# Loading q and k in blocks, placing masks by transfers and spreading softmax sums through memory, in a routed-attention kernel

## The chip, the cores and the metric

The kernel runs on one core of a Trainium2 chip. A core has a matrix engine (TensorE, in the profile PE, with its weight loads as PEld), a vector engine (VectorE, DVE), a scalar engine (ScalarE, ACT), a general engine (GpSimd, POOL) and a queue engine (SyncE, SP) that here issues nearly all transfers between device memory and on-chip memory. Each engine works through its own instructions in order and waits on semaphores for the others. The metric is the device time of one execution in microseconds (us).

## The reference

An attention block is followed by a feed-forward block. Attention has batch 4, 8 heads, sequence 768, head dimension 64. Every query and every key is assigned to the nearest of 16 centroids by cosine similarity, and a query sees only keys of its own cluster:

```python
q_assign = np.argmax(np.einsum('bhsd,hcd->bhsc', q_n, c_n), axis=-1)
k_assign = np.argmax(np.einsum('bhsd,hcd->bhsc', k_n, c_n), axis=-1)
mask = q_assign[:, :, :, None] == k_assign[:, :, None, :]
scores = scale * np.matmul(q, k.transpose(0, 1, 3, 2))
scores = np.where(mask, scores, -1000000000.0)
scores = scores - np.max(scores, axis=-1, keepdims=True)
attn = np.exp(scores)
attn = attn / (np.sum(attn, axis=-1, keepdims=True) + 1e-09)
return np.matmul(attn, v).astype(np.float32)
```

The heads are joined to rows of 512, and the second block computes `x + relu(layernorm(x) * g @ w_ch1) @ w_ch2` with a hidden width of 2048, for 4 x 768 rows.

## The kernel before, in words

The attention stage works on 16 pairs of heads (batch b, pair pr; `pairs`, numbered n). The two heads of a pair lie in the lower and the upper 64 partitions. For each pair there are 12 steps (two halves of 384 queries by six blocks of 128 keys), two steps to a "slot", so six slots (0 to 5) to a pair. In every slot PE computes the scores of two steps (L348: mask products in bf16, then q times k in float32, into `s_ps`), ACT takes the exponential (L341, `e`, five buffers), PE weighs v by the exponentials of two earlier steps (L360, `a_ps`), and DVE adds the exponentials up (`es`, L374 and L377). Scores run one slot ahead: in slot 5 of pair n they already are those of pair n+1, and need its masks.

Around this core the next pair is prepared, slot by slot, in an order written out in the loop (a manual schedule for PE, DVE and ACT; the transfers on SP are placed by the framework's scheduler):

- slot 5 of pair n-2 (for q) and slot 0 of pair n-1 (for k), `prep_transpose`: PE turns six 128 x 128 blocks of the loaded side (L243, `qk_ps`), and ACT copies the two halves out (L249) into `t0` or `t1`. Behind it the next load of that side is issued (L92, `q_sb` and `k_sb`, one buffer each), so that load waits until PE has read the buffer.
- slot 1, `prep_sims`: PE multiplies with the centroids (L260, `sim_ps`); slot 2, `prep_turn` and `prep_route`: PE turns the similarities (L276), DVE finds each token's best centroid (L285) and writes the one-hot rows (L287).
- slot 4, `prep_onehot`: PE turns the one-hot rows (L302, `oh_ps`, 128 partitions in four groups of 32: q and k of both heads), and ACT copies each group to its place in the mask tiles: plain for q (L316), scaled and shifted by a huge number for k (L314).

The pair before is finished alongside, by `finish(n-1, part)`: in slot 1 PE sums `es` over the keys (L397, `den_ps`), ACT copies the result (L405, `dsb`), and four transfers spread one row each over 32 partitions (L407, `rdens`); in slot 3 DVE takes the reciprocal (L409), which is written out as a row (L411, `row`) and read back to all partitions of its head (L419, `rb`); in slot 5 DVE multiplies (L426, `x`), turns 32 x 32 blocks (L433, `y`), and both are written out (L427, L436).

DVE also converts the weights from 64-bit words (`split_weight` and `join_weight`, L209 to L231): two chunks per pair for the first ten pairs, in slots 0 and 3, joined in the slot after, and one per pair from pair 10 on, in slot 0. Statistics of the first batch's rows (L464, L465) run on DVE in pairs 5 to 8, their use (L493, L495) in pairs 10 to 13. The feed-forward stage follows; in it PE runs from end to end.

Of the kernel before, what the change touches and what calls it, by code (L numbers as in the profile page):

```python
# [8 lines left out]
F32 = mybir.dt.float32  # L9
BF16 = mybir.dt.bfloat16  # L10
U32 = mybir.dt.uint32
I32 = mybir.dt.int32
AF = mybir.ActivationFunctionType
# [6 lines left out]
def kernel(  # L20
# [11 lines left out]
    nc = tc.nc  # L32
    B, H, S, D = q.shape
    NCL = centroids.shape[1]
    DM, FF = moe_w_ch1.shape
    P = 128
    NT = S // P
    NHALF = 2
    TH = NT // NHALF
    HC = TH * P  # L40
    Q = 32
# [4 lines left out]
    FAR = 2.0 ** 100  # L46
    WIDE = 1.0e20

    const = ctx.enter_context(tc.tile_pool(name="const", bufs=1))
# [9 lines left out]
    loads = pool("loads", 1)  # L59
    heads = pool("heads", 2)  # L60
    route = pool("route", 1)
    conv = pool("conv", 1)
    attn = pool("attn", 2)
    dram = ctx.enter_context(tc.tile_pool(name="dram", bufs=4, space=bass.MemoryType.DRAM))
# [8 lines left out]
    pairs = [(b, pr) for b in range(B) for pr in range(NPAIR)]  # L73
    loaded = {n: {} for n in range(len(pairs))}

    def load(n, names):
        if n >= len(pairs):
            return
        b, pr = pairs[n]
        for name in names:  # L80

            shape = [P, 2, NT, D] if name == "v" else [P, NT, 2, D]
            t = loads.tile(
                shape, F32, tag=name, name=f"{name}_sb", bufs=2 if name == "v" else 1
            )

            parts = 1 if n or name == "v" else NHALF
            for g in range(parts):
                cs = slice(g * NT // parts, (g + 1) * NT // parts)
                for j in range(2):  # L90
                    queue = nc.scalar if parts > 1 and j else nc.sync
                    queue.dma_start(  # L92
                        out=t[:, j] if name == "v" else t[:, cs, j, :],
                        in_={"q": q, "k": k, "v": v}[name][b, 2 * pr + j].rearrange(
                            "(p c) d -> p c d", p=P
                        )[:, cs, :],
                    )
            loaded[n][name] = t
# [24 lines left out]
    for m in mask[0] + mask[1]:  # L123
        nc.gpsimd.memset(m, 0.0)
    hits = const.tile([P, B * NPAIR], F32, name="hits")
    far = const.tile([P, 1], F32, name="far")
    nc.gpsimd.memset(far, -FAR)

    DE = HC // Q
    rdens = const.tile([P, B * NPAIR, DE], F32, name="rdens")  # L130
# [105 lines left out]
    def prep_transpose(n, side):  # L236
        src = loaded[n]["qk"[side]]
        t_sb = heads.tile([P, S], F32, tag=f"t{side}", name=f"t{side}")
        prepared[n][side] = t_sb
        for g in range(NHALF):  # L240
            t = ps("qk_ps")
            for c in range(TH):
                nc.tensor.transpose(  # L243
                    t[:, c * P : (c + 1) * P],
                    src[:, g * TH + c, :, :].rearrange("p h d -> p (h d)"),
                    ident,
                )
            if g == 0 or n:
                nc.scalar.copy(t_sb[:, g * HC : (g + 1) * HC], t[:, :HC])  # L249
            else:  # L250
                nc.vector.tensor_copy(t_sb[:, g * HC : (g + 1) * HC], t[:, :HC])
# [45 lines left out]
    def prep_onehot(n):  # L297
        t = ps("oh_ps", BF16, 1024)
        for g in range(NHALF):
            for c in range(TH):  # L300
                o = (g * TH + c) * P
                nc.tensor.transpose(  # L302
                    t[:, o : o + P],
                    onehot[:, c, g, :, :, :].rearrange("p s j d -> p (s j d)"),
                    identb,
                )

        for side in range(2):
            m = mask[n % 2][side]
            for j in range(2):  # L310
                src = t[(side * 2 + j) * Q : (side * 2 + j + 1) * Q, :S]
                dst = m[j * D : j * D + Q, :]
                if side:
                    nc.scalar.activation(dst, src, AF.Identity, bias=far[:Q], scale=FAR)  # L314
                else:
                    nc.scalar.copy(dst, src)  # L316
            prepared[n]["m", side] = m

# [69 lines left out]
    def finish(n, part):  # L390
        b, pr = pairs[n]
        if part == 0:
            den = ps("den_ps")
            for j in range(2):
                for g in range(NHALF):
                    r = (j * NHALF + g) * Q
                    nc.tensor.matmul(  # L397
                        den[r : r + Q, :HC], ones, sums[n, g][:, j, :],
                        start=True, stop=True, tile_position=(0, r),
                    )  # L400
            if n + 1 < len(pairs):
                dsb = last.tile([P, HC], F32, tag="dsb", name="dsb", bufs=1)
            else:
                dsb = late["all"][:, 1, :HC]
            nc.scalar.copy(dsb, den[:, :HC])  # L405
            for r in range(0, P, Q):
                nc.sync.dma_start(out=rdens[r : r + Q, n, :], in_=dsb[r : r + 1, :])  # L407
        elif part == 1:
            nc.vector.reciprocal(rdens[:, n, :], rdens[:, n, :])  # L409
            row = dram.tile([2, S], F32, tag="row", name="row")  # L410
            nc.sync.dma_start(  # L411
                out=row.rearrange("j (p e) -> (j p) e", e=DE), in_=rdens[:, n, :]
            )
            if n + 1 < len(pairs):
                rb = last.tile([P, S], F32, tag="rb", name="rb", bufs=1)
            else:
                rb = late["all"][:, 2]
            for j in range(2):
                nc.sync.dma_start(  # L419
                    out=rb[j * D : (j + 1) * D, :],  # L420
                    in_=row[j : j + 1, :].to_broadcast([D, S]),
                )
            late[n] = rb
        else:
            x = xs.pop(n)
            nc.vector.tensor_tensor(x, x, late.pop(n), ALU.mult)  # L426
            nc.sync.dma_start(out=xT_d[b][pr], in_=x)  # L427

            if n + 1 < len(pairs):
                y = last.tile([P, S], F32, tag="y", name="y")  # L430
            else:
                y = late["all"][:, 2]
            nc.vector.transpose(y, x)  # L433
            for i in range(P // Q):
                m = pr * P + i * Q
                nc.sync.dma_start(  # L436
                    out=x_d[b].rearrange("t (a r) m -> r (t a) m", r=Q)[:, :, m : m + Q],
                    in_=y[i * Q : (i + 1) * Q].rearrange("r (g f) -> r g f", f=Q),
                )
# [4 lines left out]
    rows = {}  # L444
# [117 lines left out]
    with tc.manual_schedule(engines=order):  # L562
        prep_transpose(0, 0)
        load(1, "q")
        turn_centroids()
        prep_transpose(0, 1)
        load(1, "k")
        prep_sims(0)
        scores(0, "qk", ("qk",))
        prep_turn(0)  # L570
        scores(1, "qk", ("qk",))
        prep_route(0)
        prep_transpose(1, 0)
        load(2, "q")
        load_weight(0)
        load_weight(1)
        prep_onehot(0)
        scores(0, "qk", ("mask", "exp"))
        scores(1, "qk", ("mask", "exp"))
        for u in range(len(pairs) * slots):  # L580
            n, slot = divmod(u, slots)
            nxt = n + 1 < len(pairs)
            if slot == 1:
                load(n + 1, "v")
            if slot == 0 and nxt:
                prep_transpose(n + 1, 1)
                load(n + 2, "k")
            if slot == 1 and nxt:
                prep_sims(n + 1)
            if slot == 2 and nxt:  # L590
                prep_turn(n + 1)
                prep_route(n + 1)
            if slot == 4 and nxt:
                prep_onehot(n + 1)
            if slot == 5 and n + 2 < len(pairs):
                prep_transpose(n + 2, 0)
                load(n + 3, "q")
            if slot == 1 and n:
                finish(n - 1, 0)
            for i in (2 * u + 2, 2 * u + 3):  # L600
                if i < len(steps):
                    scores(i)
            weigh(2 * u)
            weigh(2 * u + 1)
            if slot == 3 and n:
                finish(n - 1, 1)
            if slot == 5 and n:
                finish(n - 1, 2)
            if (n, slot) in convert:
                split_weight(convert[n, slot])  # L610
            if (n, slot - 1) in convert:
                join_weight(convert[n, slot - 1])
                load_weight(convert[n, slot - 1] + 2)
            for job in extra.pop((n, slot), ()):
                job()
# [446 lines left out]
```

## Time and profile before

| | us |
|---|---|
| median of 3 runs | 979.47 (978.92 to 980.03) |
| the profiled execution | 979.16 |
| its span in the trace | 977.4 |
| PE busy | 954.9 |
| DVE busy | 640.4 |
| ACT busy | 329.7 |

The profiled time is the device's own; the span runs from the first instruction of the trace to the last. The chain of waits is followed back from the last instruction: 90% of it lies on PE. Busy time is the sum over a whole execution, and attention and feed-forward use the engines differently, so the shares are to be read stage by stage. The attention stage ends at about 390 us. Of the weights, transfers and other rows of the page the prediction shows what it uses.

### The profile page before, as it was taken

Reading aid. Unit: us, or ns where it says so; the run is one execution under the profiler, and the core shown is the slowest. Engines: PE = TensorE matmul, PEld = TensorE weight load, DVE = VectorE, ACT = ScalarE, POOL = GpSimd, SP = SyncE. Lnnn points to the kernel's source line nnn. Section 1 sums busy time; section 2 is a strip of 40 time slices with the busy share of each in tenths; the row PEclk is TensorE's granted clock in tenths of the full one; section 3 lists DMA queues with packets and bytes.
Section 4 is the critical chain, followed back from the end, with each engine's and each line's share of the span. In section 5 each row is a group of like instructions: output and inputs, shape, how many; then the busy total and the mean of one; then the engine's idle time right before and its main releaser. Section 6 shows DMA issues by size and latency. Waiting matters only on the chain.

```text
span 977.4 us, 12727 instructions
## 1 busy us (share of the span) xinstructions
PE 954.9 (98%) x4758; PEld 593.5 (61%) x4758; DVE 640.4 (66%) x1206; ACT 329.7 (34%) x525; POOL 4.9 (1%) x31
## 2 busy tenths in 40 slices
PE   5999999999999999999999999999999999999997
PEld 3444444444444443556888556888556888556886
DVE  2788888998877777799874455653455564455431
ACT  4666676677676676222000221000211000221000
POOL 2000000000000000000000000000000000000000
PEclk9999999999999999999999999999999999999999
DMA  6346656665654422432542000212000221000011
GB/s 162 88 126 167 171 156 188 165 170 153 153 141 119 119 73 60 113 98 75 171 119 72 6 0 1 97 60 71 0 1 6 92 69 62 1 1 6 28 39 40
DMA packets 141445, 84.01 MB, mean 86 GB/s; under 512 B 110608, under 2 KB 127040, under 8 KB 141376
## 3 DMA queue, kind: packets, MB, share of 16 engines
q1 hardware_dynamic: 139104, 82.70, 30.5%
q8 instruction: 39, 0.64, 0.3%
q10 hardware_dynamic: 2272, 0.43, 0.2%
q14 instruction: 30, 0.25, 0.1%
HBM read 64.00 MB, written 19.00 MB: 85 GB/s over the span
## 4 chain that ended last, share of the span: by engine, by line
PE 90%; ACT 5%; issue 2%; DVE 1%; DMA 1%; ACTq 0%; SPq 0%; DVEq 0%
PE x_ps L737 17%; PE x_ps L652 17%; PE s_ps L348 14%; PE a_ps L360 12%; PE z_ps L737 8%; PE z_ps L652 8%; PE y_ps L737 4%; PE y_ps L652 4%; ACT mask_0k L314 1%; ACT mask_1k L314 1%; PE qk_ps L243 1%; ACT e L341 1%; PE sim_ps L260 1%; PE den_ps L397 1%; DMA q_sb<-in_q_dram 1%
## 5 line engine op out<-in xcount | busy, mean ns | idle before, releaser
L341 ACT ACTIVATE e<-s_ps 128x768 f32<-128x768 f32 x192 | 151.8, 817 | 55.2 <-PE s_ps L348 51.7
L348 PE MATMUL s_ps<-t,t 64*128 64x384 f32 x768 | 156.9, 487 | 0.0
L377 DVE TENSOR_TENSOR es<-es,e 128x768 f32<-128x768 f32 x128 | 122.3, 955 | 39.0 <-ACT e L341 32.4
L360 PE MATMUL a_ps<-e,v_sb 128*64 128x384 f32 x768 | 144.8, 499 | 0.0
L360 PEld LDWEIGHTS a_ps<-e,v_sb 128*64 128x64 f32 x768 | 46.7, 136 | 86.4 <-issue 86.3
L737 PE MATMUL x_ps<-w2t,h 128*128 128x256 f32 x384 | 84.5, 379 | 0.0
L348 PEld LDWEIGHTS s_ps<-t,t 64*128 64x128 f32 x768 | 69.4, 190 | 19.8 <-issue 19.7
L737 PEld LDWEIGHTS x_ps<-w2t,h 128*128 128x128 f32 x384 | 72.7, 190 | 10.1
L667 ACT COPY u<-x_ps 128x384 f32<-128x384 f32 x64 | 30.7, 479 | 134.2 <-PE x_ps L652 134.2
L667 ACT COPY p<-x_ps 128x384 f32<-128x384 f32 x32 | 15.3, 479 | 139.3 <-PE x_ps L652 139.3
L530 DVE TENSOR_TENSOR ws<-w 128x256 f32<-128x256 f32 x64 | 24.8, 418 | 53.3 <-PE z_ps L652 53.3
L748 DVE TENSOR_TENSOR o_sb<-x_ps,xb 128x256 f32<-128x256 f32 x48 | 20.2, 420 | 54.5 <-PE x_ps L737 54.5
L672 DVE TENSOR_TENSOR h<-z_ps,u 128x384 f32<-128x384 f32 x64 | 35.2, 550 | 22.4 <-ACT u L667 13.8
L652 PE MATMUL x_ps<-xn,w 128*128 128x384 f32 x128 | 46.6, 487 | 0.6 <-ACT late L386 0.6
L652 PE MATMUL z_ps<-xt,ws 128*128 128x384 f32 x128 | 46.6, 487 | 0.0
L652 PE MATMUL x_ps<-xt,w 128*128 128x384 f32 x128 | 46.6, 487 | 0.0
L652 PE MATMUL x_ps<-xt,ws 128*128 128x384 f32 x128 | 46.5, 486 | 0.0
L652 PE MATMUL x_ps<-xn,ws 128*128 128x384 f32 x128 | 46.5, 486 | 0.0
L652 PE MATMUL y_ps<-xn,w 128*128 128x384 f32 x128 | 46.5, 486 | 0.0
L652 PE MATMUL z_ps<-xn,ws 128*128 128x384 f32 x128 | 46.5, 486 | 0.0
L737 PE MATMUL x_ps<-w,h 128*128 128x256 f32 x192 | 42.7, 379 | 0.0
L737 PE MATMUL y_ps<-w,h 128*128 128x256 f32 x192 | 42.1, 379 | 0.0
(130 smaller groups left out, 1309.0 us busy)
## 6 DMA issues: line engine op xcount, KB each, us to landing
raw<-in_moe_w_ch_dram SPq DMA_DIRECT2D x32, 512.0 KB, 3.9
v_sb<-in_v_dram SPq DMA_DIRECT2D x32, 192.0 KB, 3.8
xn<-xT_d SPq DMA_DIRECT2D x16, 384.0 KB, 4.7
xr<-x_d SPq DMA_DIRECT2D x24, 256.0 KB, 3.3
xb<-x_d SPq DMA_DIRECT2D x48, 128.0 KB, 2.2
out_dram<-o_sb SPq DMA_DIRECT2D x48, 128.0 KB, 1.7
q_sb<-in_q_dram SPq DMA_DIRECT2D x30, 192.0 KB, 3.9
k_sb<-in_k_dram SPq DMA_DIRECT2D x30, 192.0 KB, 3.5
```

The source lines that it names most:

```text
L243: nc.tensor.transpose(t[:, c * P : (c + 1) * P], src[:, g * TH + c, :, :].rearrange("p h d -> p (h d)"), ident,)
L314: nc.scalar.activation(dst, src, AF.Identity, bias=far[:Q], scale=FAR)
L341: nc.scalar.activation(e, s[:, :, :HC], AF.Exp, scale=SCALE)
L348: nc.tensor.matmul(s[:, j, :HC], of_keys[rows[j], keys], of_queries[rows[j], cols], start=part == first, stop=part != first, skip_group_ch ...
L360: nc.tensor.matmul(acc[j * D : (j + 1) * D, :HC], loaded[n]["v"][:, j, c, :], e[:, j, :], start=(c == 0), stop=(c == NT - 1),)
L377: nc.vector.tensor_tensor(es, es, soft.pop(i), ALU.add)
L530: nc.vector.tensor_tensor(t[:, i], x, y, op)
L652: nc.tensor.matmul(bank[:, :HC], lhs[:, c, :], rhs[:, c, :], start=first and c == 0, stop=c == NDH - 1, skip_group_check=True,)
L667: nc.scalar.copy(t, bank[:, :HC])
L672: nc.vector.tensor_tensor(h, bank[:, :HC], other, ALU.add)
L737: nc.tensor.matmul(bank[:, :MH], hidden[lhs + (c,)][:, tt * P : (tt + 1) * P], rhs[:, c, :], start=first and c == 0, stop=c == NFH - 1, sk ...
L748: nc.vector.tensor_tensor(o, bank[:, :MH], x, ALU.add)
```

## The change

Three things change, all in the attention stage, and one call moves.

1. `load_blocks`: k of pairs 1 to 15 and q of pairs 10 to 15 (21 sides) are loaded by four transfers, each of 32 partitions by 24 runs of 32 numbers (128 bytes), so that a DVE transpose of 32 x 32 blocks gives the same `t0` or `t1` that PE and ACT gave. Before, a side was loaded by two transfers in runs of 256 bytes. For these sides `prep_transpose` is one DVE instruction.
2. `prep_onehot` copies all 128 partitions out in one ACT instruction, with a bias and a scale that differ by partition (`far` has two columns now), and four transfers put 16 rows each in the mask tiles. It is called in slot 3 instead of slot 4.
3. `finish`, part 0: the four rows are written to device memory by one transfer (`flat`), and read back by a second one to 128 partitions by 12.

```diff
+    blocks = {(n, name) for n in range(1, len(pairs)) for name in ("qk" if n >= 10 else "k")}
+
+    def load_blocks(n, name):
+        b, pr = pairs[n]
+        t = loads.tile([P, S], F32, tag=name, name=f"{name}_sb")
+        for i in range(P // Q):
+            nc.sync.dma_start(
+                out=t[i * Q : (i + 1) * Q].rearrange("f (t a r) -> f t a r", t=NT, r=Q),
+                in_={"q": q, "k": k}[name][b, 2 * pr + i * Q // D].rearrange(
+                    "(a f t) d -> f t a d", f=Q, t=NT
+                )[:, :, :, i * Q % D : i * Q % D + Q],
+            )
+        loaded[n][name] = t
...
+        if (n, "qk"[side]) in blocks:
+            nc.vector.transpose(t_sb, src)
+            return
...
+        m = route.tile([P, S], BF16, tag="m", name="m")
+        nc.scalar.activation(m, t[:, :S], AF.Identity, bias=far[:, 0:1], scale=far[:, 1:2])
         for side in range(2):
-            m = mask[n % 2][side]
             for j in range(2):
-                src = t[(side * 2 + j) * Q : (side * 2 + j + 1) * Q, :S]
-                dst = m[j * D : j * D + Q, :]
-                if side:
-                    nc.scalar.activation(dst, src, AF.Identity, bias=far[:Q], scale=FAR)
-                else:
-                    nc.scalar.copy(dst, src)
-            prepared[n]["m", side] = m
+                o = (side * 2 + j) * Q
+                nc.sync.dma_start(
+                    out=mask[n % 2][side][j * D : j * D + NCL, :], in_=m[o : o + NCL, :]
+                )
+            prepared[n]["m", side] = mask[n % 2][side]
...
-            for r in range(0, P, Q):
-                nc.sync.dma_start(out=rdens[r : r + Q, n, :], in_=dsb[r : r + 1, :])
+            flat = dram.tile([P // Q, HC], F32, tag="flat", name="flat")
+            nc.sync.dma_start(out=flat, in_=dsb[0:P:Q, :])
+            nc.sync.dma_start(
+                out=rdens[:, n, :], in_=flat.rearrange("i (p e) -> (i p) e", e=DE)
+            )
...
-            if slot == 4 and nxt:
+            if slot == 3 and nxt:
                 prep_onehot(n + 1)
```

The framework's scheduler places the transfers on SP. In the built programs the transfers issued while pair 4 runs stand in this order, before and after:

```
before: rdens x4, raw, xn, row, rb x2, raw, q_sb x2, xT_d, x_d x4, k_sb x2, v_sb x2
after:  flat, raw, mask q, rdens, mask q, mask k x2, q_sb, row, q_sb, xn, rb x2, raw,
        v_sb x2, xT_d, x_d x4, k_sb x4
```

More of the change, by code (lines that the diff above doesn't have):

```diff
@@ L80, in load @@
         for name in names:
+            if (n, name) in blocks:
+                load_blocks(n, name)
+                continue
             shape = [P, 2, NT, D] if name == "v" else [P, NT, 2, D]
@@ L125 @@
     hits = const.tile([P, B * NPAIR], F32, name="hits")
-    far = const.tile([P, 1], F32, name="far")
-    nc.gpsimd.memset(far, -FAR)
+    far = const.tile([P, 2], F32, name="far")
+    for rows, bias, scale in ((slice(0, D), 0.0, 1.0), (slice(D, P), -FAR, FAR)):
+        nc.gpsimd.memset(far[rows, 0:1], bias)
+        nc.gpsimd.memset(far[rows, 1:2], scale)
     DE = HC // Q
```

## The prediction

> **What bounds the kernel now.** I read the busy shares first, then the chain that ended last, then one attention pair on the timeline, and last the transfer queue. The whole-kernel shares say that TensorE (PE) is busy 98% of the time. They are an average over two stages, and only the attention stage (to about 390 us) is touched.
>
> ```profile
> PE 954.9 (98%) x4758; PEld 593.5 (61%) x4758; DVE 640.4 (66%) x1206; ACT 329.7 (34%) x525; POOL 4.9 (1%) x31
> DVE  2788888998877777799874455653455564455431
> ```
>
> The reader should see that VectorE (DVE), which gets new work, is 80 to 90% busy in slices 3 to 11, far above its mean of 66%. The chain of waits then shows one "turn" (first mask product of a pair to that of the next):
>
> ```profile
> 112.04 1.79 PE s_ps L348 x12
> 113.83 1.44 PE a_ps L360 x8
> 115.27 0.81 PE qk_ps L243 x6
> ...
> 119.24 0.78 PE sim_ps L260 x8
> 120.02 0.65 PE den_ps L397 x8
> ...
> 123.83 0.48 PE simT_ps L276 x3
> ...
> 135.41 1.79 PE s_ps L348 x12
> ```
>
> A turn is 135.41 - 112.04 = 23.37 us, nearly all PE. On the timeline (starts up to 0.07 earlier) it splits into six score steps of 1.72, six weighings of 1.44, turning k 0.81, similarities and denominators 1.43, their turn back 0.48, one-hot 0.44, turning q 0.88, and a wait of 0.37: sum 23.37. DVE and the queue in that turn:
>
> ```profile
> 114.94 0.98 DVE L433 STREAM_TRANSPOSE y<-x 128x768 f32<-128x768 f32 x1
> 115.84 0.92 DVE L374 TENSOR_TENSOR es<-e 128x768 f32<-128x768 f32 x1
> 121.24 2.79 SPq L407 DMA_DIRECT2D rdens<-dsb  x4
> 124.34 0.56 DVE L285 TENSOR_REDUCE best<-simT_ps 128x24 f32<-128x384 f32 x1 [1.74 <-PE simT_ps L276]
> 128.22 0.22 DVE L409 RECIPROCAL rdens<-rdens 128x12 f32<-128x12 f32 x1
> 128.47 0.33 SPq L411 DMA_DIRECT2D row<-rdens  x1
> 129.93 1.13 SPq L419 DMA_DIRECT2D rb<-row  x2
> 135.07 0.59 SPq L92 DMA_DIRECT2D q_sb<-in_q_dram  x1
> 135.39 0.96 DVE L377 TENSOR_TENSOR es<-es,e 128x768 f32<-128x768 f32 x1 [1.16 <-ACT e L341]
> 135.41 0.34 PE L348 MATMUL s_ps<-mask_1q,mask_1k 64*128 64x384 bf16 x2 [0.37 <-ACT e L341]
> ```
>
> DVE waits only 1.74 + 1.16 = 2.90 us per turn, so it works 20.47. The reciprocal L409 runs four microseconds after its four transfers were issued, without waiting, and row leaves the queue before the next q load.
>
> **The change, part by part.**
>
> *Removed from PE.* Turning k, 0.81 in every turn. For pairs 10 on also turning q, 0.88 (two pairs ahead, so from turn 8 on). The 0.37 wait goes too: the exponential at its end stands behind four mask copies (131.11 to 134.53, 3.4 us of ScalarE), which become one of 0.90 (the 895 ns of a 768-column copy; more partitions, same columns) a slot earlier. PE alone would then need 23.37 - 0.81 - 0.37 = 22.19 us a turn, and 21.31 once q is off it as well.
>
> *Added to DVE.* A turn of one side costs 0.90, the distance from y's start to the next start above. DVE then works 21.37 of 22.19 us: it fits only if it waits less than 0.82 us per turn. So every new wait on DVE counts.
>
> *Block loads.* Each side becomes four issues of 128-byte runs instead of two of 256. The nearest row is x_d<-y, same shape outwards, 0.55 per issue and 2.6 us to landing. Bounds for the load are 2.6 and, doubling today's 3.9, 7.8. Either lies under the turn (over 20 us) between load and use: cost nothing. If that cover were gone, the DVE turn would wait for it.
>
> *Sums by two transfers.* The write to flat follows the copy of den as today and has 5 us of cover. The read rdens<-flat is what matters. In the order in which the changed kernel issues its transfers (a listing of the built program, no times) it stands behind the first mask transfer from pair 2 on, except in pair 5. That transfer waits for the mask copy, which waits for the one-hot product. So L409 waits for a product of slot 3 (of 0 to 5), and behind L409 on DVE stand the conversion of weights, four sums, the x product, y, and now the turn of k, for which PE's similarities wait. That closes a loop, similarities to similarities:
> - PE to the one-hot: 1.43 + 3.16 + 0.48 + 3.16, and 0.55 until ScalarE starts (130.56 to 131.11): 8.78.
> - Mask copy 0.90, queue 0.03, one mask issue 0.59.
> - rdens<-flat to landing: nearest below is row<-rdens (same 128 x 48 bytes, outwards) at 1.4, nearest above rb<-row (a read of rows just written, 32 times the bytes) at 3.3. I take 1.9, nearer to the row of its size.
> - DVE, from starts in the timeline: reciprocal 0.14, split 1.34, two sums 1.93, join 2.52, two sums 1.94, x 0.98, y 0.90, k 1.02: 10.77.
>
> Together 22.97, plus 0.82 for each batch-norm statistic in between (0.68 + 0.17, less overlap), plus 0.90 where q is turned on DVE too.
>
> *The q load moves past row and rb.* In the listing rb<-row stands behind the q load (pairs 2 to 6), in pairs 3 and 4 row itself as well. The q load waits until PE has turned the former q at slot 5. Similarities to there: 1.43 + 3.16 + 0.48 + 3.16 + 0.44 + 3.16 + 3.16 + 0.88 = 15.87. Then a q issue 0.59, row to rb 1.46 (128.47 to 129.93), second rb issue 0.54, landing 3.3, and x, y, k 2.90: 24.7. Bounds: row at 1.4, or 2.5 if its packets queue behind q's as some rdens rows do (1.7 to 3.8 today); I take the idle value. Where row goes first, two q issues stand ahead of rb: 15.9 + 1.2 + 0.54 + 3.3 + 2.90 = 23.85.
>
> *Masks by transfer.* Copy done at 9.7 of that loop's time, five issues of 0.58, landing 2.0 as rdens: ready at about 14.1, needed at 15 or later. Cost nothing, 0.9 of slack where q is on DVE; a landing of 3.8 would add 0.9 per turn there. In the prologue there is no slack: 0.90 + 1.74 + 2.0 against 3.43 is +1.2, less 1.47 of k on PE, plus 0.90 on DVE: +0.6 (from -0.3 to +2).
>
> [...] By stretches (PE and its weight loads, DVE, ACT, POOL busy, then the granted clock):
>
> ```profile
> 15.50:20.70 5.20, 1.86 (x16) 1.23 (x16) 0.00 (x0) 4.11 (x6) 0.00 (x0) 1.00 0.44 99
> 20.70:24.10 3.40, 3.40 (x15) 2.19 (x16) 1.80 (x3) 2.27 (x5) 0.00 (x0) 0.50 0.06 13
> ```
>
> After 5.2 us with 1.86 us of PE work the clock is halved for 3.4 us. [...]
>
> **The sum** (15 turns, number n starts with pair n):
> - turn 0: +0.6
> - turns 1, 2 at 22.19: 2 x -1.18 = -2.4
> - turn 3 at 23.85: +0.5; turns 4, 5 at 24.7: +2.7
> - turns 6, 7 at 24.7 (23.85 plus a statistic; the first loop with two gives 24.6): +2.7; turn 8 at 24.6: +1.2; turn 9 (statistic and q) at 24.7: +1.3; turn 10 at 24.2 (q, small work): +0.8, less 0.1 that before lost here
> - turns 11 to 14: one conversion (3.86) gone from the loop, so PE's 21.31 decides: 4 x -2.06 = -8.2
> - last pair and feed-forward: +0.2; one more transfer, feed-forward work of 20 us over it.
>
> Net -0.7. The profiled execution took 979.16 us (span 977.4, 1.8 around it), 0.3 under the median of 979.47. The forecast is 979.16 - 0.7, or 978.4 us: no change that can be told (0.2%, or 2 us, is about what a measurement of this kernel tells from none).
>
> **Rivals.**
> - *The relief comes through* (PE decides everywhere): turns 1 to 7 at 22.19, 8 to 14 at 21.31: 7 x -1.18 + 7 x -2.06 + 0.7 = -22, 957 us. For it: 2.9 us of DVE waiting today. Against: 0.82 is left, and two new waits stand ahead of k. Partial relief ends at 960 to 970.
> - *The spread read lands late* (slower): rdens<-flat at 3.3 instead of 1.9 lengthens turns 7 to 10 by 1.4 each, and pushes turns 11 to 14 to about 22.3 (+1.0 each): +9.6, 988 us. It decides from about 2.4 (+0.5 in eight turns). For it: it is a read of rows just written, as rb is, in a queue that is busier. Against: 6 KB only.
> - *The k wait hits less often* (same side, small gain): middle turns (4 to 10) at 24.1 instead of 24.6 give 7 x -0.5, or 975.
>
> **How the numbers follow.** Cancelling as summed, 0.53 (own range 972 to 985; 0.20 faster, 0.20 same, 0.13 slower); relief 0.11; k wait rarer 0.07; late read or a tripped clock 0.29, of which 0.02 still same. So faster 0.38, same 0.22, slower 0.40. The range goes to 968 (half of the relief kept) and 991 (late read, with some row queueing).
>
> **What would show it.** Right: similarities (sim_ps) wait 1.5 to 3.4 us for the DVE turn of k in turns 3 to 10 and not in 11 to 14; L409 waits for rdens; turns of 22.2, then 24 to 25, then 21.3. Wrong: no such waits (relief), PE waiting for masks, or a granted clock below 1 in the middle turns.

## The result, and the profile after

The changed kernel takes 1010.69 us (median; 1009.92 to 1012.09) against 979.19 us of the kernel before in the same runs: a ratio of 1.0324, interval 1.0306 to 1.0341. It is 31.5 us slower. The forecast was 978.4 with a range up to 991, so both the time and the range were missed. The profiled execution took 1012.09 us (span 1010.3).

The page of the changed kernel, its busy times, the granted clock by slice, and the shares of the chain:

```profile
PE 961.8 (95%) x4632; PEld 583.1 (58%) x4632; DVE 658.6 (65%) x1227; ACT 277.6 (27%) x435; POOL 5.1 (1%) x34
PEclk9999998999999999999999999999999999999999
PE 77%; DMA 9%; DVE 8%; SPq 2%; ACT 2%; issue 1%; ACTq 0%; DVEq 0%
```

PE had 126 matmuls fewer (4632 against 4758) and was still busy 6.9 us longer: some of them ran at a granted clock of 0.50, and in the turns with a wait the similarities run in two parts, as shown below. Before, 90% of the chain that ended last lay on PE and 1% on transfers; now it is 77% and 9%, with 8% on DVE. The waits of PE and of DVE say where (us in total, times, longest):

```profile
PE sim_ps L283 <- DVE t L261: 30.7, 12, 5.3
PE s_ps L370 <- DMA mask_0k<-m: 4.5, 1, 4.5
...
DVE rdens L434 <- DMA rdens<-flat: 29.4, 11, 4.8
DVE x L451 <- DMA rb<-row: 29.2, 12, 5.6
```

DVE, which waited for no transfer inside a turn before, now stands 58.6 us at two small transfers, the read of the denominators and that of `rb`, and PE stands 30.7 us at the turn of k that is queued behind them. (In the changed kernel L261 is DVE's turn of a side, L283 the similarities, L434 the reciprocal, L451 and L458 x and y, L336 the mask transfers, L429 and L430 the write and the read of the denominators, L436 row, L444 rb, L83 and L110 the loads.)

By turn, in us (forecast: the prediction's; half clock: an estimate, half of PE's busy time in the stretches of granted clock 0.50 behind the wait):

| turn | forecast | measured | wait for the turn of k | lost to half clock |
|---|---|---|---|---|
| 0 | 23.1 | 22.59 | | |
| 1, 2 | 22.19 | 22.13, 22.13 | | |
| 3 | 23.85 | 25.03 | 2.08 | |
| 4, 5 | 24.7 | 30.65, 30.35 | 5.33, 4.68 | 2.5, 2.8 |
| 6, 7 | 24.7 | 27.96, 27.97 | 3.37, 3.58 | 1.7, 1.5 |
| 8, 9 | 24.6, 24.7 | 26.33, 27.83 | 2.58, 3.80 | 1.7, 1.4 |
| 10 | 24.2 | 23.60 | 1.45 | |
| 11 | 21.31 | 26.19 | 2.41 | 1.7 |
| 12, 13, 14 | 21.31 | 22.72, 22.72, 22.45 | 0.57, 0.58, small | |

The turns together took 380.65 us, 31.8 more than the forecast's 348.9. Of these 13.3 are half clock, by that estimate; 18.5 are a turn of k that comes later than forecast. The start was 1.4 us later than before, the rest of the kernel 0.7 longer.

The column of waits counts idle time alone, and a turn with a wait is some 0.8 us longer still. PE runs the similarities of q, has nothing more to do until k is turned, and then runs those of k; before, they ran side by side. So turn 3, at a granted clock of 1.00, has 22.95 us of PE work against 22.13 in turns 1 and 2, and with its wait of 2.08 that makes 25.03. Turns 4 to 7 have 22.85 to 22.89 us of work once the half clock is taken off, which agrees.

Turn 4 shows the loop through rb, on the timeline:

```profile
112.79 0.62 SPq L110 DMA_DIRECT2D q_sb<-in_q_dram  x1
113.46 0.64 SPq L436 DMA_DIRECT2D row<-rdens  x1
114.14 0.59 SPq L110 DMA_DIRECT2D q_sb<-in_q_dram  x1
114.78 0.64 SPq L474 DMA_DIRECT2D xn<-xT_d  x1
116.31 1.12 SPq L444 DMA_DIRECT2D rb<-row  x2
122.30 0.96 DVE L451 TENSOR_TENSOR x<-x,rb 128x768 f32<-128x768 f32 x1 [4.64 <-DMA rb<-row]
123.29 0.98 DVE L458 STREAM_TRANSPOSE y<-x 128x768 f32<-128x768 f32 x1
124.20 0.94 DVE L261 STREAM_TRANSPOSE t<-k_sb 128x768 f32<-128x768 f32 x1
125.19 0.85 PE L283 MATMUL sim_ps<-t,cT 128*32 128x384 f32 x2 [5.33 <-DVE t L261]
```

The q loads and xn stand ahead of rb, as forecast; the two rb reads, issued from 116.31 on, had landed at 122.3, 5.4 us after the second issue, where the kernel before shows 3.3. The stretches in which rb is under way, before, in this turn and in turn 9 (length, busy times, clock, busy share of the transfer engines, GB/s):

```profile
129.90:134.30 4.40, 4.40 (x33) 1.84 (x30) 4.13 (x6) 3.29 (x5) 0.00 (x0) 1.00 0.27 91
```

```profile
116.30:122.30 6.00, 3.56 (x22) 1.08 (x18) 1.25 (x2) 1.77 (x3) 0.00 (x0) 1.00 0.91 272
256.60:260.50 3.90, 3.90 (x28) 1.87 (x26) 3.69 (x7) 2.25 (x4) 0.00 (x0) 1.00 0.31 103
```

The transfer engines were 27% busy under the old rb and 91% under this one. The wait of turn 9, where rb is not behind q, shows the other loop; it starts in turn 8, which ends at 255.96:

```profile
245.61 0.38 SPq L220 DMA_DIRECT2D raw<-in_moe_w_ch_dram  x1
250.75 0.58 SPq L336 DMA_DIRECT2D mask_1q<-m  x1
251.43 0.53 SPq L430 DMA_DIRECT2D rdens<-flat  x1
254.89 0.23 DVE L434 RECIPROCAL rdens<-rdens 128x12 f32<-128x12 f32 x1 [4.80 <-DMA rdens<-flat]
264.41 0.95 DVE L451 TENSOR_TENSOR x<-x,rb 128x768 f32<-128x768 f32 x1
266.30 0.94 DVE L261 STREAM_TRANSPOSE t<-k_sb 128x768 f32<-128x768 f32 x1
267.29 0.85 PE L283 MATMUL sim_ps<-t,cT 128*32 128x384 f32 x2 [3.80 <-DVE t L261]
```

SP stood almost five microseconds (from 245.99 to 250.75) at the mask transfer, which waits for ACT's copy; the read of the denominators was issued behind it, and DVE reached its reciprocal 3.5 us after that issue. Everything behind L434 on DVE moved with it, down to the turn of k.

And the half clock. The trace records a granted clock of 0.50 behind seven of the waits for the turn of k: for 6.83 us from 123.28 and from 154.00 (turns 4 and 5), and for 3.41 us from 184.72, 212.03, 239.34, 266.64 (turns 6 to 9) and 317.84 (turn 11). Stretches of turns 4, 10 and 11 (columns as above, PE busy first, the clock third from the end):

```profile
119.87:123.28 3.41, 0.00 (x0) 0.00 (x0) 0.96 (x1) 0.00 (x0) 0.00 (x0) 1.00 0.79 272
123.28:126.70 3.42, 1.51 (x10) 0.58 (x12) 3.37 (x5) 0.00 (x0) 0.00 (x0) 0.50 0.70 179
126.70:130.10 3.40, 3.40 (x15) 1.42 (x12) 3.26 (x6) 1.33 (x3) 0.00 (x0) 0.50 0.89 138
290.50:293.95 3.45, 2.00 (x18) 0.55 (x16) 3.42 (x5) 0.49 (x2) 0.00 (x0) 1.00 0.98 192
314.43:317.84 3.41, 1.00 (x12) 0.40 (x12) 3.41 (x5) 0.01 (x1) 0.00 (x0) 1.00 0.79 188
317.84:321.25 3.41, 3.41 (x14) 1.45 (x12) 3.27 (x6) 1.55 (x3) 0.00 (x0) 0.50 0.85 136
```

Behind the stretch without PE work (from 119.87) and the one with 1.00 us of it (turn 11) the clock was 0.50; behind the one with 2.00 us (turn 10) it stayed at 1.00. In turn 4, where the wait reaches into the half clock, PE was busy for 1.51 us of its first 3.42 and the clock was 0.50 for another 3.40; in turn 11 PE was busy all through the 3.41 us, and the clock behind them was 1.00.

### The profile page after: what moved, and what is told of

Same layout as the page of the kernel before. It is cut to its first block, busy times and chain, and to the rows that moved or that the text cites. A ratio compares the mean times of both kernels' runs of the same rounds, so it can differ in the third digit from the quotient of the medians.

```text
span 1010.3 us, 12513 instructions
## 1 busy us (share of the span) xinstructions
PE 961.8 (95%) x4632; PEld 583.1 (58%) x4632; DVE 658.6 (65%) x1227; ACT 277.6 (27%) x435; POOL 5.1 (1%) x34
## 4 chain that ended last, share of the span: by engine, by line
PE 77%; DMA 9%; DVE 8%; SPq 2%; ACT 2%; issue 1%; ACTq 0%; DVEq 0%
PE x_ps L762 16%; PE x_ps L677 16%; PE s_ps L370 9%; PE z_ps L762 8%; PE z_ps L677 8%; PE a_ps L382 7%; PE y_ps L762 4%; PE y_ps L677 4%; DVE es L399 2%; DMA q_sb<-in_q_dram 2%; DMA rdens<-flat 2%; DMA raw<-in_moe_w_ch_dram 2%; PE sim_ps L283 2%; PE den_ps L419 1%; DMA rb<-row 1%
## 5 line engine op out<-in xcount | busy, mean ns | idle before, releaser
L370 PE MATMUL s_ps<-t,t 64*128 64x384 f32 x768 | 161.7, 500 | 0.0
L370 PEld LDWEIGHTS s_ps<-t,t 64*128 64x128 f32 x768 | 71.9, 197 | 24.0 <-issue 24.0
L283 PE MATMUL sim_ps<-t,cT 128*32 128x384 f32 x128 | 28.3, 577 | 30.8 <-DVE t L261 30.7
```

The costliest lines, as they stand in the source:

```text
L283: nc.tensor.matmul(sim[r : r + Q, :HC], cT[:, pr, :, :].rearrange("p j c -> p (j c)"), prepared[n][side][:, g * HC : (g + 1) * HC], start= ...
L370: nc.tensor.matmul(s[:, j, :HC], of_keys[rows[j], keys], of_queries[rows[j], cols], start=part == first, stop=part != first, skip_group_ch ...
```

## Experiments

**Theory 1:** the work is cheap enough, but the turn of k stands on DVE behind x and the reciprocal, which now wait for small transfers that stand behind other things on SP's queue; the half clock behind such waits adds to it. **Theory 2:** the work itself is too much: DVE full, loads in small pieces slow, or SP's many issues too long. Each run is compared with the kernel before, measured beside it (979.0 to 979.8 us).

### The parts one by one

`no_blocks` keeps the masks by transfer and the two-transfer sums, and loads and turns all sides as before; `blocks_only` is the reverse (masks, sums and the slot of `prep_onehot` as before).

```diff
-    blocks = {(n, name) for n in range(1, len(pairs)) for name in ("qk" if n >= 10 else "k")}
+    blocks = set()
```

> The changed kernel without its first part: all sides of q and k loaded whole and turned by PE as before; masks by one copy and transfers in slot 3, sums by two transfers. Theory 1, the two other parts do no harm as long as no turn stands on VectorE: the 0.37 us wait of 14 turns goes, the prologue loses 1 to 2: 973 to 978 us. Theory 2, the transfers of masks and sums are what costs: over 985 us.

> The first part of the change alone: 21 sides in blocks and turned on VectorE, masks by four copies in slot 4 and sums by four transfers as before. Theory 1, the turn of k behind x, and x behind rb, is enough for the loss because the scheduler again puts rb behind the loads of q (and from pair 10 on row behind a load of v): waits of sim_ps in most turns, 1000 to 1035 us. Theory 2, the loss needs the read rdens<-flat behind the mask transfers: no waits over 1 us, 958 to 970 us.

Measured: `no_blocks` 974.57 us (ratio 0.995, 0.9934 to 0.9967), in theory 1's range, turns of 22.93; `blocks_only` 1058.21 us (1.0802, 1.0779 to 1.0825). So masks and sums together are a small gain, 0.44 us a turn, and the blocks carry the loss. `blocks_only` was also worse than the whole change, further than I had expected. Its waits:

```profile
DVE x L447 <- DMA rb<-row: 77.1, 11, 9.7
PE sim_ps L281 <- DVE t L259: 58.8, 11, 8.3
```

```profile
SPq L110 <- PE a_ps L381: 74.0, 6, 14.6
```

The last line is SP's: a load of v waits for its buffer, until PE has used the v before, and in turns 9 to 14 of this program the scheduler had put `row` behind that load. The same DVE instruction is late for another reason, also an order on SP's queue.

### The same instructions, transfers in written order

`sp_written` takes nothing away; SP joins the engines whose order is the program's.

```diff
-    order = {mybir.EngineType.PE, mybir.EngineType.DVE, mybir.EngineType.Activation}
+    order = {mybir.EngineType.PE, mybir.EngineType.DVE, mybir.EngineType.Activation, mybir.EngineType.SP}
```

> Same instructions as the changed kernel, but the transfers on SP are issued in the written order of the loop (rdens in slot 1, masks, row and rb in slot 3, the q load in slot 5) instead of the scheduler's. Theory 1, the order of the queue puts rdens, row and rb late, and the turn of k on VectorE stands behind them: the waits of sim_ps for the turn of k (30 us in 13 turns now) all but go, turns of 22.1 and then 21.3 us, full clock after the prologue, 956 to 962 us. Theory 2, VectorE has too little room (21.4 of 22.2 us) and the longer landings alone are enough: waits of over 1 us stay in most turns, over 980 us.

Measured: 982.78 us (1.0029, 1.0014 to 1.0043). 28 of the 31 us go by order alone, which is theory 1's direction; theory 2's number (over 980) held too, because more than 20 us of the expected relief did not come. PE's waits in the attention stage show why:

```profile
PE s_ps L370 <- DMA mask_0k<-m: 10.3, 2, 8.2
PE s_ps L370 <- DMA mask_1k<-m: 5.6, 2, 5.0
PE sim_ps L283 <- DVE t L261: 1.4, 3, 0.6
```

The wait for the turn of k has shrunk from 30.7 to 1.4 us. Now mask transfers are late, behind loads: 8.2 us at the start, 2.1 and 5.0 us at the ends of turns 5 and 10, each with half clock behind it (a mean granted clock of 0.85 in turn 0, 0.93 in turn 6, 0.89 in turn 11).

### Needless work ahead of the similarities

```diff
-                nc.tensor.matmul(
+                for _ in range(9 if 4 <= n <= 12 and side == 0 else 1):
+                    nc.tensor.matmul(
...
```

> The changed kernel, with 3.1 us of needless matrix work (16 repeated products of the q side's similarities, overwritten) ahead of the similarities of k in turns 3 to 11, where PE waits now. Theory 1, the halved clock after those waits costs about 15 us of its own: the halved stretches after the prologue (31 us in seven turns) go, 992 to 999 us, although PE has more to do. Theory 2, the clock does not matter because VectorE's chain sets the pace: 1008 to 1015 us.

Measured: 1051.18 us (1.0732, 1.0714 to 1.075). The run missed its aim. I had sized the filler by the four similarities of a pair (eight records in the profile), which run side by side in 0.67 us. Nine that write the same group of 32 partitions run one after another: turns 3 to 7 were 31.81 us, which is 22.13 + 9.68, or 0.605 for each of the 16 extra ones, and not 3.1 for all (turns 8 to 11, without the turn of q on PE, were 31.0 to 31.3):

```profile
112.00:143.81 31.81, 31.81 (x187) 12.97 (x183) 20.66 (x32) 13.24 (x20) 0.00 (x0) 1.00 0.51 124
```

PE is busy throughout, at a granted clock of 1.00: with that much room no transfer and no DVE instruction made it wait in turns 3 to 11. It doesn't separate the half clock from the waits, as it was meant to. The order on SP differed too (rb ahead of q), so nothing more is drawn from it.

### The turn of k ahead of x

`k_early` moves the turn of k from slot 0 of the pair before to slot 5 of the one before that, beside that of q, ahead of x and y.

```diff
-            if slot == 0 and nxt:
+            if slot == 0 and n == 0:
...
                 prep_transpose(n + 2, 0)
                 load(n + 3, "q")
+                prep_transpose(n + 2, 1)
+                load(n + 3, "k")
```

> The changed kernel with VectorE's turn of k moved from the first step of a pair to the last step of the pair before, ahead of x and y, which wait for rb. Theory 1 (the 31 us are PE waiting for a turn of k that stands behind x's wait for rb): the 30 us of waits ahead of the similarities in turns 3 to 13 go, and with them the stretches at half clock; VectorE's own work of 22 to 24 us sets those turns: 962 to 978. Theory 2 (it is not the place of the turn: the transfers of k and q in pieces land late, or VectorE has too much work): the wait moves to the den products or to the turn itself, 990 or more.

Measured: 991.38 us (1.0127, 1.0109 to 1.0146). The time lies in theory 2's range, at its edge, but the wait is not where theory 2 put it. The similarities wait no more, as theory 1 says, and what is queued next behind x, the one-hot rows, takes their place:

```profile
PE oh_ps L325 <- DVE onehot L310: 19.1, 9, 3.6
```

```profile
DVE rdens L434 <- DMA rdens<-flat: 20.1, 12, 3.2
DVE x L451 <- DMA rb<-row: 18.9, 11, 4.9
```

DVE's standing at the two transfers is the cause, and the turn of k was only the first thing behind it. In turns 12 and 13 this kernel reached 21.32 us.

### Masks off SP's queue

`masks_pool` issues the mask transfers from GpSimd, in the scheduler's order otherwise; `spw_masks_pool` does it with SP in written order.

```diff
-                nc.sync.dma_start(
+                nc.gpsimd.dma_start(
                     out=mask[n % 2][side][j * D : j * D + NCL, :], in_=m[o : o + NCL, :]
                 )
```

> The changed kernel with the four mask transfers of a pair issued by GpSimd instead of SyncE, so that the read of the denominators no longer stands behind a transfer that waits for ScalarE's copy of the masks. Theory 1a (that place in the queue, the loop through masks, denominators, x and the turn of k, makes most of the waits): turns 9 to 14 fall from 145 us together to about 134, and turns 3 to 8 keep some of theirs from rb behind q: 975 to 1000. Theory 1b (the place of rb behind the loads of q, v and xn alone is enough to keep VectorE late): within 8 us of 1010 or above it.

> SyncE's transfers in their written order and the masks from GpSimd: no small transfer stands behind a load, and no mask behind a wait. Theory 1: what the run in written order still lost (mask products waiting 8.2, 2.1 and 5.0 us, with the half clock behind them) goes; turns of 22.2 throughout: 955 to 966. Theory 2 (the parts together give no more than the masks and sums alone, 974.6): 972 or more.

Measured: `masks_pool` 1065.02 us (1.0868, 1.085 to 1.0887), `spw_masks_pool` 977.51 us (0.9974, 0.9958 to 0.9991). The first fell on theory 1b's side, and far beyond: rb stayed behind the loads of q in turns 4 to 8, and in turns 9 to 14, with the masks gone, the scheduler put a v load ahead of row, and SP stood at it:

```profile
SPq L110 <- PE a_ps L382: 74.4, 8, 14.5
```

So a queue's order can't be changed here at one place alone. The second lies in theory 2's range and above theory 1's, but not for theory 2's reason: its turns 10 and 12 to 14 were 21.32 us, PE's floor, but 8.5 us were still waited for masks at the start, and up to 3.3 us for the turn of k, as DVE still stood 7.8 us at rb and 6.7 at the denominators.

### Loads in whole rows

`spw_rows_dve` is `sp_written` with the 21 sides loaded by two transfers in runs of 256 bytes. DVE turns what it finds, so that q and k are out of order, and only the time is of use.

```diff
-            if (n, name) in blocks:
-                load_blocks(n, name)
-                continue
...
-            nc.vector.transpose(t_sb, src)
+            nc.vector.transpose(t_sb, src.rearrange("p a b c -> p (a b c)"))
```

> Written order as before, masks on SyncE, but the 21 sides are loaded in whole rows by two transfers, as the kernel before loads them, and VectorE turns what it finds, so that q and k are not the reference's: the turn costs the same, only the form of the load differs. Theory 1 (the pieces of 128 bytes cost SyncE's time, four issues instead of two, and nothing else): 2 us less on the queue ahead of the masks, whose waits shrink: 970 to 980 against 982.8. Theory 2 (small pieces slow every other transfer): 955 to 966.

Measured: 977.93 us (0.9983, 0.9973 to 0.9992), a step of 0.9983 against 1.0029, or 4.5 us. That lies in theory 1's range. Which part of the 4.5 us is SP's shorter issue and which the transfer engines' was not separated.

### x and y two slots later

`x_late` moves x and y of a pair from slot 5 to slot 1 of the next pair, two slots on (the expectation calls them steps).

```diff
-            if slot == 5 and n:
+            if slot == 1 and n > 1:
+                finish(n - 2, 2)
+            if slot == 5 and n + 1 == len(pairs):
                 finish(n - 1, 2)
```

> The changed kernel with one move: x and y of a pair (VectorE's product with rb and its turn) come two steps later, behind the next turn of k and its similarities, instead of right ahead of it; the transfers stay in the order that the scheduler gives them. Theory 1 (the waits of PE come from the turn of k standing behind x, which waits for rb): the 30 us of waits and the stretches at half clock of the middle turns go, also the loop through masks and denominators, since the masks no longer hang on x: 957 to 972. Theory 2 (SyncE's queue, with its 14 to 18 us of issues in a turn, is late by itself, and something else of it reaches PE): 985 or more, with PE waiting for masks, one-hots or den products.

Measured: 967.06 us (0.9881, 0.9864 to 0.9897), in theory 1's range: this move of two DVE instructions and their five transfers is worth 43.6 us against the changed kernel and makes a gain of 12 us out of the loss. PE's and DVE's waits in the attention stage, and the landing of rb (KB each, median us):

```profile
PE s_ps L370 <- DMA mask_0k<-m: 6.3, 2, 4.3
...
DVE rdens L434 <- DMA rdens<-flat: 1.2, 1, 1.2
...
DVE x L451 <- DMA rb<-row: 0.3, 1, 0.3
```

```profile
rb<-row SPq DMA_DIRECT2D x30, 192.0 KB, 5.5
```

rb lands no sooner than in turn 4 of the changed kernel, 5.5 us after its issue, and in most turns a load of q still stands ahead of it; nobody waits for it. DVE's 58.6 us at transfers are 1.5. The same work on DVE fits, which speaks against theory 2: turns 1 to 4 took 22.13 us and turns 12 to 14 21.32. The run changes more than one thing, though, not one as its expectation says: the scheduler re-sorted SP's queue. The denominators' read now stands ahead of the masks, which opens the other loop as well, and ahead of rb stands one issue of a q load at most, where in turns 3 to 7 of the changed kernel there are two. What each of these is worth was not taken apart; the next run bears on the denominators.

### Sums as before

`sums_before` is the changed kernel with the four transfers `rdens<-dsb` of the kernel before.

```diff
-            flat = dram.tile([P // Q, HC], F32, tag="flat", name="flat")
-            nc.sync.dma_start(out=flat, in_=dsb[0:P:Q, :])
-            nc.sync.dma_start(
-                out=rdens[:, n, :], in_=flat.rearrange("i (p e) -> (i p) e", e=DE)
-            )
+            for r in range(0, P, Q):
+                nc.sync.dma_start(out=rdens[r : r + Q, n, :], in_=dsb[r : r + 1, :])
```

> The changed kernel without its third part: the denominators are read by four transfers, as before. If the spread by two transfers is what puts the loop in place (the second transfer waits for the first, and stands behind a mask transfer), this is faster than the changed kernel: 980 to 1000. If four issues cost SyncE more than the second landing (blocks alone, with four reads and no mask transfers, took 1058), it is slower: 1010 to 1040.

Measured: 998.51 us (1.0192, 1.0175 to 1.0209), in the first range. DVE's two waits, and PE's:

```profile
DVE x L448 <- DMA rb<-row: 40.0, 10, 6.1
...
DVE rdens L431 <- DMA rdens<-dsb: 3.9, 3, 2.8
PE sim_ps L283 <- DVE t L261: 21.0, 11, 3.9
```

The reciprocal's wait falls from 29.4 to 3.9 us, that of x grows from 29.2 to 40.0, and 12 us of time go. The scheduler put the four reads ahead of the masks here, so form and place changed together. The place seems to count: in `x_late` the read by two transfers stands ahead of the masks too, and DVE waits 1.2 us for it. So the part that spreads the sums costs 12 us in the changed kernel's order, where with no blocks it is part of a gain, and rb alone is enough for PE to wait 21 us.

### The start, and the cures together

`spw_m0` (written order) and `x_late_m0` (x and y later, scheduler's order) copy the masks of pair 0 by ACT as before; `spw_m0_pool_xlate` has written order, the other masks from GpSimd, and x and y later.

```diff
+        if n == 0:
+            for side in range(2):
+                m = mask[0][side]
+                for j in range(2):
+                    o = (side * 2 + j) * Q
+                    nc.scalar.activation(
+                        m[j * D : j * D + Q, :], t[o : o + Q, :S], AF.Identity,
+                        bias=far[o : o + Q, 0:1], scale=far[o : o + Q, 1:2],
+                    )
+                prepared[n]["m", side] = m
+            return
```

> Transfers in their written order, and the masks of pair 0 alone copied by ScalarE as the kernel before does, without transfers. The run in written order waited 8.2 us for pair 0's masks and ran the first 10 us of the turns at half clock, where the kernel before has its first mask product 5 us earlier. If that is all of the loss at the start, 982.8 falls by 5 to 9 us: 973 to 978. If the start is lost elsewhere (loads of pair 1 in pieces), 980 or more.

> All cures together: written order, pair 0's masks copied, the other masks from GpSimd's queue, x and y two steps later. Theory 1: turns of 22.1 to turn 9 and 21.3 to 22 after it, no long wait: 950 to 960. Theory 2 (SyncE's issues or the landing of loads set a floor of their own): 968 or more.

> The changed kernel with x and y two steps later, and with the masks of pair 0 copied by ScalarE without transfers, as the kernel before does. If the 4.3 us for which the first mask product waits for pair 0's masks, and the later start of the turns (21.2 us against 19.4 before), come from these transfers, 967 falls by 2 to 4 us: 963 to 965. If the start is held by the loads of pair 1, 966 to 968.

Measured: `spw_m0` 977.02 us (0.9976, 0.9966 to 0.9985), 5.2 less than `sp_written` by the ratios, as expected; its turn 1 begins 5.3 us earlier. `x_late_m0` took 963.87 us (0.9845, 0.9829 to 0.9862), 3.5 less than `x_late` by the ratios. That is the size expected, but in part by luck: turn 1 begins only 0.9 us earlier, and the rest comes from the middle turns, most of it from the clock. At the end of turn 5 PE waits 2.0 us for a mask in `x_late` and 1.5 in `x_late_m0`; behind the first the clock was 0.50 from 157.32 to 160.73, behind the second it stayed at 1.00. Turn 6 of `x_late`, then of `x_late_m0`:

```profile
156.34:180.29 23.95, 23.95 (x152) 10.36 (x153) 19.89 (x34) 12.67 (x18) 0.00 (x0) 0.93 0.67 157
154.93:177.25 22.32, 22.32 (x153) 9.75 (x154) 20.08 (x34) 12.61 (x18) 0.00 (x0) 1.00 0.72 164
```

The same work, without a wait in either, takes 1.63 us longer with 3.41 us at half clock; half of PE's busy time in these is 1.71.

`spw_m0_pool_xlate` took 971.1 us (0.9913, 0.9897 to 0.993), in theory 2's range (968 or more). Its turns 11 to 14 were 21.32 us, but new waits came: 3.7 us of PE at one-hots, and 5.0 us in turn 10 behind ACT's copy of x:

```profile
272.29 0.48 ACT L419 COPY x<-a_ps 128x384 f32<-128x384 f32 x1 [7.74 <-DMA xT_d<-x]
```

ACT waits until the x before has been written out, and in written order SP issued that transfer at 269.66, behind the loads of q, k and v and the two transfers of the denominators. So SP's queue set a floor here, as theory 2 says. `x_late_m0` is the fastest version that was run, 15 us under the kernel before.

## Why the prediction was wrong, point by point

The steps that failed are three terms of the sum and one that it does not have: the landing of rb behind the loads of q (3.3 us taken, 5.4 measured), the landing of the denominators' read (1.9 taken, 3.5 measured), turns 11 to 14, where rb was left out (7.1 us), and the half clock, for which the sum has nothing (13.3 us).

- *Relief of PE* (22.19 and 21.31 us a turn): right. Turns 1 and 2 took 22.13; turns 12 to 14 of `x_late` and `k_early` took 21.32 or up to 0.44 more.
- *The two loops*: right as mechanism. The waits are those named, for the turn of k (30.7 us in 12 turns), behind L434 and L451, and undoing any of their parts moves the time. The sizes were not.
- *rb behind the q load, 24.7 us with a landing of 3.3*: the term that failed is the landing. It was taken from a stretch in which the transfer engines were 27% busy; here they were 91% busy and it took 5.4. Without the half clock turns 4 and 5 came to 28.2 and 27.5, 6.3 us over the forecast together, and turns 3, 6 and 7 are 4.5 over.
- *The read of the denominators, landing 1.9*: turn 9 shows 3.5 from issue to reciprocal, the rival's 3.3. Turns 8 to 10 are 1.2 us over, without the half clock. The rival "late read" had the mechanism and counted 1.4 a turn for it; the chance that it got was too low.
- *Turns 11 to 14, where one conversion less was to let PE decide, -8.2*: failed. x still waits for rb there (1.86 us in turn 11) with the turn of k behind it. The conversion's 3.86 us shorten DVE's work, but not a wait that starts with a transfer issued late. Turn 11 took 26.19, turns 12 to 14 about 22.6: 7.1 us over, and 1.7 of half clock.
- *The clock kept out of the sum*: the largest single failure, 13.3 us. Behind seven of the waits for the turn of k, those of 2.41 to 5.33 us, the granted clock was 0.50; behind those of turns 3 and 10, 2.08 and 1.45 us, it stayed at 1.00. The waits forecast were of 1.5 to 3.4 us. The stretch of the kernel before that the prediction shows (15.50 to 20.70) was a warning: in its last 3.42 us, from 17.28, PE was busy for 0.68, and half clock followed.
- *Masks by transfer, nothing; start +0.6*: right for the turns of the changed kernel, where PE waited for a mask only at the start. Turn 1 began 1.5 us later than before, inside the range given (-0.3 to +2). With the loops open the masks do surface in later turns: 2.0 us of wait at the end of turn 5 of `x_late`, and a clock of 0.50 behind it.
- *Block loads, nothing*: the turn over load and use does hide their landing, but not what they do to others on the same queue: 4.5 us in written order (`spw_rows_dve`).
- *Range and chances*: "a late read or a tripped clock" ended at 988 and 991 as if only one could come. The two go together: a late landing lengthens the wait, and of the waits for the turn of k in the changed kernel those of 2.41 us and more had half clock behind them, those of up to 2.08 had not. Added, 978.4, the 9.6 of the late read and the 13.3 of half clock are 1001.3, and with rb's landing at its size under load the measured time is in sight.

What stays open: the 13.3 us of half clock are worked out from busy time at clock 0.50. Turn 6 of `x_late` and `x_late_m0` bears out the price of one stretch of 3.41 us, but no run shows the changed kernel without its stretches at half clock. Nor was it shown what decides whether half clock follows a wait. And the effects of position and queue order in `x_late` were not taken apart.

## What to carry to other kernels

When work is moved to an engine that has slack on average, look at what it will be queued behind: an instruction that waits for a small transfer makes everything after it late (DVE stood 58.6 us at two such transfers, PE 30.7 at the turn of k behind them), and putting two such instructions two slots later, with the queue order that came of it, was worth more than the change itself. Where a scheduler orders the transfers, every edit re-sorts the queue; list the order, and price each landing by how busy the transfer engines are in that stretch, not by an idle one (rb took 3.3 us at 27% and 5.4 at 91%). Look for half clock behind a wait in the profile of the kernel before, and where waits are forecast, give it a term in the sum; here it was 13.3 us.

## What the runs showed of the hardware

- In the changed kernel the granted clock was 0.50 for 3.41 or 6.83 us behind the seven waits for the turn of k of 2.41 to 5.33 us, and stayed at 1.00 behind those of 2.08, 1.45 and 0.58 us. The length of the wait alone does not tell the two apart over all runs: behind 2.0 us (for a mask, at the end of turn 5) the clock of `x_late` was 0.50.
- A read of 192 KB (`rb`) landed 3.3 us after its issue with the transfer engines 27% busy (the kernel before), and 5.4 us after it with 91% (turn 4 of the changed kernel).
- The four similarities of a pair, which write four different groups of 32 partitions, take 0.67 us together (119.17 to 119.84 in the kernel before); repeated into the same group, each extra one added 0.605 (`fill_pe`).
